# RWKV-7 recurrence and a mixture of 16 experts on one core: expert places of different widths, filled in order of the experts' counts

## The chip, the core and the metric

The kernel runs on one core of a Trainium2 chip. The core has a matrix engine (TensorE; PE in the profile, its weight loads PEld), three engines for element work (VectorE: DVE, ScalarE: ACT, GpSimd: POOL), a queue engine that starts loads and stores (SyncE: SP), and 16 DMA engines that move the data. Each engine works through its own list of instructions in order and waits on semaphores for the others. Matmuls read SBUF and write PSUM, 8 banks of 2 KB a partition. The metric is device time in microseconds, the median of several executions. All data are fp32; an fp32 matmul is recorded as two passes, each with its own weight load.

## The reference

First a recurrence over 768 steps for 4 x 8 heads of size 40, then a layer of 16 experts (4 groups of 4) over the 3072 tokens it gives. Each token goes to one expert, the best of its best group.

```python
for t in range(S):
    y[:, :, t] = np.einsum('bhd,bhde->bhe', rt, state)
    Sa = np.einsum('bhde,bhe->bhd', state, at)
    state_decay = state * wt[:, :, None, :] - np.einsum('bhd,bhe->bhde', Sa, bt)
    state = state_decay + np.einsum('bhd,bhe->bhde', vt, kt)
x = y.transpose(0, 2, 1, 3).reshape(B * S, H * D)        # 3072 x 320
g_idx = argmax(x @ w_group);  e_idx = argmax(xg @ w_expert[g])
h = np.maximum(xg[mask_e] @ w1[g, e], 0.0)               # 320 -> 1024
out[tok_idx] = (g_w * e_w)[:, None] * (h @ w2[g, e])     # 1024 -> 320
```

## The kernel before, in words

The first part (to about 420 us of the profile) computes the recurrence in chunks of 128 steps, 6 chunks, and writes x to memory (`x_nat`). While it runs, tokens are assigned: `choose` finds each token's expert (one-hot rows `oh`) and weight (`pay`), `rank_products` and `ranks` number the tokens within their expert, `table` and `table_products` turn this into a table `tab` that holds for each expert and each row the token's number and its weight, and `index` makes integers of it (`src_i` for gathering, `dst_i` for storing). `lift` sees to it that each expert has at least a first tile of 128 rows counted. The last of the six chunks is assigned in the tail.

In the second part, the tail, each of the 16 experts has a place of 240 rows: a first tile of 128 and a second of 112 (`CAP`, `TB2`, `WX`). Rows that no token fills are computed and not stored. Tokens beyond the 240th of an expert are marked in `ov`; if any is, or a guard of the recurrence trips, a slow path behind the tail (line 1154) runs, which is skipped in the profiled execution.

For expert e: `gather` (line 743, POOL) fetches the rows of x; `fill` (749, ACT) copies a remainder of 64 columns once more, so that it stands on both halves of the partitions; `turn_x_in` (755 to 758) transposes on PE and copies to `xTs`; `layer1` multiplies with w1: x has 320 = 128 + 128 + 64 columns, so line 772 does the two full parts for eight blocks of 128 hidden units, and line 780 the part of 64, two blocks at a time on the two row halves. The moving operand has the place's width, 240 columns, in a call. Half of the outputs get their relu on ACT (782), half on DVE (783). `layer2` then does for each of the two tiles eight matmuls of 320 columns (793), a scaling by the weight on DVE (799) and an indirect store (800, POOL).

The order on each engine is the order in which the program is written (lines 1061 to 1129). Experts 0 and 1 are interleaved with the assignment of the last chunk: `layer1(0, 0, P, "whole")` is the part of line 772 for expert 0's first tile, "rest" that of line 780. From expert 2 on a loop runs: gathers for e + 2, fills for e + 1, `layer1(e)`, transposes for e + 1, `layer2` for both tiles, weights for e + 3. Weights (2.62 MB an expert) are loaded by `load_weights` on SP into three buffers in turn; the loads wait until PE has read the buffer's last user. Experts come in the order 0 to 15.

PSUM banks are handed out in turn from two rings, "wide" (5 banks) and "thin" (3).

## Time and profile before

| | |
|---|---|
| median of 3 runs | 730.04 us (727.44 to 734.29) |
| profiled execution, device time | 731.19 us |
| its span, first to last instruction | 729.5 us |
| PE busy | 624.9 us (86% of the span) |
| PE weight loads busy | 533.2 us (73%) |
| DVE / ACT / POOL busy | 361.4 / 276.7 / 294.6 us |
| memory read and written | 74.41 and 9.50 MB |
| mean granted clock of PE | 0.941 of 2.4 GHz |

A row of the timeline is: start in us, duration in us, engine, line, operation, output <- inputs, shape, how many instructions were merged into the row, and in brackets the idle time before it and what ended it. A row of the windows view gives for each engine the busy time in a stretch and the number of instructions, then PE's granted clock as a share of 2.4 GHz, the share of time in which the DMA engines were busy, and the rate. The view of a line gives minimum, median and maximum duration in ns of all instructions of one program line. Matmuls overlap, so that the time of a pass is read from start to start and not from its own duration.

### The profile page before, as it was taken

The numbers are of one execution on the slowest core, as the hardware profiler recorded it, in microseconds if no ns is written. First come the engines' busy times: TensorE is split into PE (matmuls) and PEld (weight loads), VectorE is DVE, ScalarE is ACT, GpSimd is POOL, SyncE is SP. The second block draws the span as 40 slices with busy tenths as digits, with TensorE's granted clock in tenths as the row PEclk, the third lists the DMA queues.
The fourth block names the chain that finished last, engine by engine and source line by source line (L and its number), as shares of the span: only waits on it lengthen the run. The fifth ranks groups of instructions, "written<-read, shape, count | busy, mean of one in ns | idle before, by whom it ended". The sixth has DMA issues, their size and how long they took to land. (4 is left out here: it accounts for less than half of the span.)

```text
span 729.5 us, 26775 instructions
## 1 busy us (share of the span) xinstructions
PE 624.9 (86%) x11850; PEld 533.2 (73%) x11850; DVE 361.4 (50%) x631; ACT 276.7 (38%) x720; POOL 294.6 (40%) x415
## 2 busy tenths in 40 slices
PE   2642888888899889988879899999999999999993
PEld 2532777787788778877878786877777777777772
DVE  8799588778678778776714442111111111111110
ACT  6952966575685774762260310111111111111100
POOL 5110089779779879868200013222222222222111
PEclk9755689999999999999999999999999999999997
DMA  5540414245345344442253064755555555554000
GB/s 130 124 111 1 97 29 99 58 120 123 94 113 128 60 111 96 122 137 42 40 174 85 22 190 132 241 176 175 178 178 176 176 174 175 178 179 165 14 13 15
DMA packets 129103, 84.74 MB, mean 116 GB/s; under 512 B 77995, under 2 KB 121008, under 8 KB 128980
## 3 DMA queue, kind: packets, MB, share of 16 engines
q1 hardware_dynamic: 125908, 74.10, 36.9%
q0 software_dynamic: 3072, 8.85, 3.5%
q8 instruction: 95, 1.56, 0.9%
q14 instruction: 28, 0.23, 0.1%
HBM read 74.41 MB, written 9.50 MB: 115 GB/s over the span
## 5 line engine op out<-in xcount | busy, mean ns | idle before, releaser
L800 POOL DMA_INDIRECT out_dram<-homek,dst_i x32 | 31.8, 992 | 212.6 <-DVE homek L799 203.4
L481 POOL TENSOR_TENSOR home<-home,tmp 128x30 f32<-128x30 f32 (+9 forms) x150 | 110.3, 735 | 11.7
L479 POOL TENSOR_TENSOR tmp<-home,TT 128x30 f32<-128x30 f32 (+9 forms) x150 | 93.6, 624 | 11.4
L419 PE MATMUL nar<-home,home 64*128 64x128 f32 x768 | 69.0, 323 | 31.8 <-DVE home L387 15.0
L772 PE MATMUL nar<-homeg,home 128*128 128x240 f32 (+2 forms) x464 | 90.3, 347 | 0.0
L419 PEld LDWEIGHTS nar<-home,home 64*128 64x128 f32 x768 | 59.7, 224 | 37.4 <-issue 23.0
L772 PEld LDWEIGHTS nar<-homeg,home 128*128 128x128 f32 x464 | 79.0, 191 | 9.1 <-issue 3.3
L743 POOL DMA_INDIRECT homeq<-x_nat,src_i x32 | 31.2, 976 | 92.9 <-DVE pad L644 66.6
L543 PE MATMUL seq<-VN,homeg 64*64 64x40 f32 x768 | 50.8, 236 | 14.2 <-ACT RHS L547 9.4
L431 ACT COPY TT<-nar 32x256 f32<-32x256 f32 x96 | 34.7, 361 | 72.0 <-PE nar L419 37.7
L543 PEld LDWEIGHTS seq<-VN,homeg 64*64 64x64 f32 x768 | 44.4, 141 | 17.0 <-ACT RHS L547 10.7
L793 PE MATMUL one<-home,homeq 128*128 128x320 f32 (+1 forms) x192 | 53.4, 434 | 0.0
L799 DVE TENSOR_SCALAR homek<-one,tab 128x320 f32<-128x320 f32 (+1 forms) x22 | 12.1, 551 | 81.2 <-PE one L793 81.2
L545 PE MATMUL seq<-ST,home 64*64 64x40 f32 x768 | 50.2, 234 | 0.0
L592 DVE TENSOR_TENSOR MN<-nar,up 128x512 f32<-128x512 f32 x48 | 31.0, 687 | 36.6 <-PE nar L588 36.5
L793 PEld LDWEIGHTS one<-home,homeq 128*128 128x128 f32 (+1 forms) x192 | 34.8, 184 | 15.7 <-issue 0.3
L426 DVE TENSOR_TENSOR homeg<-nar,up 64x256 f32<-64x256 f32 x80 | 33.4, 418 | 24.5 <-ACT TT L432 14.5
L545 PEld LDWEIGHTS seq<-ST,home 64*64 64x64 f32 x768 | 44.6, 144 | 0.0
L793 PE MATMUL one<-home,DT 128*112 128x320 f32 (+1 forms) x160 | 44.5, 433 | 0.0
L782 ACT ACTIVATE DT<-nar 128x480 f32<-128x480 f32 (+1 forms) x13 | 7.5, 573 | 93.7 <-PE nar L780 62.5
L462 POOL TENSOR_SCALAR_AFFINE_SELECT TT<-TT 128x1024 f32<-128x1024 f32 x6 | 8.9, 1479 | 82.5 <-DVE TT L458 78.4
L782 ACT ACTIVATE homeq<-nar 128x480 f32<-128x480 f32 (+2 forms) x12 | 6.8, 570 | 91.0 <-PE nar L780 75.4
(209 smaller groups left out, 1291.2 us busy)
## 6 DMA issues: line engine op xcount, KB each, us to landing
home<-in_w_dram SPq DMA_DIRECT2D x16, 1280.0 KB
home<-in_w_dram SPq DMA_DIRECT2D x16, 1024.0 KB
home<-in_w_dram SPq DMA_DIRECT2D x32, 128.0 KB
home<-in_kT_dram SPq DMA_DIRECT2D x48, 80.0 KB
home<-in_bT_dram SPq DMA_DIRECT2D x48, 80.0 KB
home<-in_aT_dram SPq DMA_DIRECT2D x24, 160.0 KB
VN<-in_v_dram SPq DMA_DIRECT2D x48, 80.0 KB
home<-in_vT_dram SPq DMA_DIRECT2D x48, 80.0 KB
```

Of the source, the lines that this page charges most:

```text
L419: nc.tensor.matmul(ps[j][:, i, :], lhsT=KB[half(j), i0 + i, c2], rhs=At[half(j), 0:b + 1:b, :], start=True, stop=True)
L426: nc.vector.tensor_tensor(G[half(j), hs], ps[j][half(j), :, HW:], up2[half(j), None, :].broadcast_to([HW, NH, HW]), op=ALU.mult)
L431: nc.scalar.copy(out=TT[q:q + HB, ns], in_=ps[j][q:q + HB, :, HW:])
L479: eng.tensor_tensor(t3, W[:, r0:r2, s:s + 1].broadcast_to([P, m, n]), sub[:, s:s + 1, s + 1:].broadcast_to([P, m, n]), op=ALU.mult)
L481: eng.tensor_tensor(W[:, r0:r2, s + 1:], W[:, r0:r2, s + 1:], t3, op=ALU.subtract)
L543: nc.tensor.matmul(ps[half(1 - j), i, :], lhsT=self.G[half(j), i, :], rhs=self.VN[half(j), i, j, :], start=True, stop=False)
L545: nc.tensor.matmul(ps[half(1 - j), i, :], lhsT=self.At[half(j), 1 + 2 * i + self.c2, :], rhs=S0[half(j), i, :], start=False, stop=True)
L592: nc.vector.tensor_tensor(self.MN[:, j], ps[j], up2[:, None, :].broadcast_to([P, NI, HW]), op=ALU.mult)
L743: nc.gpsimd.indirect_dma_start(out=xt[:CAP[h], :DM], out_offset=None, in_=x_nat[:, :], in_offset=bass.IndirectOffsetOnAxis(ap=src_i[:CAP[h ...
L772: nc.tensor.matmul(ps[:, f, :], lhsT=w1s[:, ko, (g0 + f) * P:(g0 + f + 1) * P], rhs=xT[:, ko, :], start=(f == 0 and ko == 0), stop=False, ...
L793: nc.tensor.matmul(ps, lhsT=hts[e % 2][:, f, h * P:h * P + n], rhs=wbuf[e % 3][2][:, f, :], start=(k == 0), stop=(k == FQ - 1))
L800: nc.gpsimd.indirect_dma_start(out=out[:, :], out_offset=bass.IndirectOffsetOnAxis(ap=dst_i[:n, h, e:e + 1], axis=0), in_=yt[:n], in_offse ...
```

## The change

Places from the third on are no longer tied to an expert. Experts 0 and 1 keep the first two places; the other 14 are sorted by their number of tokens while the kernel runs, and fill places 2 to 15 in falling order. Each place has its own width, a constant of the program: 240 for places 0, 1 and 2, then 232, twice 224, twice 216, twice 208, and 192 for the last six. The second tile of a place has its width less 128 rows. In places of 192 it has 64, and there the eight matmuls of the second layer go alternately to output partitions 0 to 63 and 64 to 127 of one bank, two separate sums that ACT and DVE add afterwards.

What this needs is new code: `seen_by(NN)` counts all tokens, `order_experts` ranks the 14 experts by count (a matmul with ones, seven operations on DVE) and writes their numbers to `er_v`; `sort_tables` sorts the columns of `tab`; `overflow` computes `ov` from the widths; `load_expert` reads an expert's number from `er_v` into a register of SP, from which the loads' addresses are formed. The load for the third place, which stood at the head of the tail, stands behind `order_experts`. `ranks` has one operation less.

```diff
-    TB2 = 112
+    NF0 = 2
+    NV = NE - NF0
+    WIDTHS = [240] * (NF0 + 1) + [232] + [224] * 2 + [216] * 2 + [208] * 2
+    WIDTHS += [192] * (NE - len(WIDTHS))
...
-        for i, x in enumerate((0, P, P + TB2)):
-            nc.gpsimd.memset(thr[:, i:i + 1], float(x))
+        for i, x in enumerate(WIDTHS):
+            nc.gpsimd.memset(room_k[:, i:i + 1], float(x))
...
-            nc.vector.tensor_reduce(out=rank, in_=mine, axis=AX.X, op=ALU.add)
-            nc.vector.tensor_tensor(ge, rank[:, :, None].broadcast_to([P, n, 3]),
-                                    thr[:, None, :].broadcast_to([P, n, 3]), op=ALU.is_ge)
-            nc.vector.scalar_tensor_tensor(row[:, ms], ge[:, :, 1], -float(P), rank, op0=ALU.mult, op1=ALU.add)
-            nc.vector.tensor_tensor(hs, ge[:, :, :2], ge[:, :, 1:], op=ALU.subtract)
+            nc.vector.tensor_reduce(out=rank[:, ms], in_=mine, axis=AX.X, op=ALU.add)
+            nc.vector.tensor_single_scalar(hs[:, :, 1], rank[:, ms], float(P), op=ALU.is_ge)
+            nc.vector.scalar_tensor_tensor(row[:, ms], hs[:, :, 1], -float(P), rank[:, ms], op0=ALU.mult, op1=ALU.add)
+            nc.vector.tensor_scalar(hs[:, :, 0], hs[:, :, 1], -1.0, 1.0, op0=ALU.mult, op1=ALU.add)
...
-            nc.vector.tensor_copy(out=ov[:, ms], in_=ge[:, :, 2])
...
+        def order_experts():
+            pt = spot([P, NE])
+            nc.tensor.matmul(pt, lhsT=ones, rhs=seen, start=True, stop=True)
...
+            nc.vector.scalar_tensor_tensor(key, lane[:, NF0:NE], -1.0 / NE, pt[:, NF0:], op0=ALU.mult, op1=ALU.add)
+            nc.vector.tensor_tensor(more, key[:, None, :].broadcast_to(sq_v), key[:, :, None].broadcast_to(sq_v),
+                                    op=ALU.is_gt)
+            nc.vector.tensor_reduce(out=pos, in_=more, axis=AX.X, op=ALU.add)
+            nc.vector.tensor_tensor(sel, pos[:, None, :].broadcast_to(sq_v), lane[:, :NV, None].broadcast_to(sq_v),
+                                    op=ALU.is_equal)
+            nc.vector.tensor_tensor(more, sel, lane[:, None, NF0:NE].broadcast_to(sq_v), op=ALU.mult)
+            nc.vector.tensor_reduce(out=pos, in_=more, axis=AX.X, op=ALU.add)
+            nc.vector.tensor_copy(out=er_v, in_=pos)
+
+        def sort_tables():
...
+            nc.vector.tensor_tensor(big_t.rearrange("p (a k) e -> p a k e", a=4),
+                                    tab.rearrange("p a h e -> p (a h) e")[:, :, None, NF0:].broadcast_to(n4),
+                                    sel[:, None, :, :].broadcast_to(n4), op=ALU.mult)
+            nc.vector.tensor_reduce(out=srt.rearrange("p a h k -> p (a h k)"), in_=big_t, axis=AX.X, op=ALU.add)
+            nc.vector.tensor_scalar(src_v, srt[:, 0], float(NTOK - 1), None, op0=ALU.min)
+            nc.vector.tensor_copy(out=dst_v, in_=srt[:, 0])
+
+        def overflow():
...
+        def rows_of(e, h):
+            return WIDTHS[e] - P if h else P
...
+        def layer2(e, h):
+            n = rows_of(e, h)
+            ps = room([P, DM], "thin")
+            two = n <= HW
+            for k in range(FQ):
                 f = order[k]
-                nc.tensor.matmul(ps, lhsT=hts[e % 2][:, f, h * P:h * P + n], rhs=wbuf[e % 3][2][:, f, :],
-                                 start=(k == 0), stop=(k == FQ - 1))
+                nc.tensor.matmul(ps[half(k % 2, n)] if two else ps[:n], lhsT=hts[e % 2][:, f, h * P:h * P + n],
+                                 rhs=wbuf[e % 3][2][:, f, :], start=(k < 1 + two), stop=(k >= FQ - 1 - two),
+                                 skip_group_check=two)
...
+            if two:
+                nc.scalar.copy(out=yt[:n], in_=ps[half(1, n)])
+                nc.vector.tensor_tensor(yt[:n], ps[:n], yt[:n], op=ALU.add)
+                nc.vector.tensor_scalar(yt[:n], yt[:n], wt, None, op0=ALU.mult)
+            else:
+                nc.vector.tensor_scalar(yt[:n], ps[:n], wt, None, op0=ALU.mult)
...
+        def load_expert(e):
+            if e < NF0:
+                load_weights(e * DM, e * F, wbuf[e % 3])
+                return
+            er = nc.sync.value_load(er_v[0:1, e - NF0:e - NF0 + 1], min_val=NF0, max_val=NE - 1)
+            load_weights(nc.s_assert_within(er * DM, NF0 * DM, (NE - 1) * DM),
+                         nc.s_assert_within(er * F, NF0 * F, (NE - 1) * F), wbuf[e % 3])
...
         gate["tail"] = True
-        load_weights(2 * DM, 2 * F, wbuf[2])
...
         ranks(NF, B)
+        seen_by(NN)
         table(NF, B)
         layer1(0, 0, P, "rest")
+        order_experts()
+        load_expert(2)
         layer1(1, 0, P, "whole")
         table_products(NF)
         index(1)
         for e in range(2):
             gather(e, 1)
+        sort_tables()
         gather(2, 0)
         layer1(1, 0, P, "rest")
         layer2(0, 0)
+        overflow()
...
-            layer1(e, 0, WX)
+            layer1(e, 0, WIDTHS[e])
...
-                load_weights((e + 3) * DM, (e + 3) * F, wbuf[e % 3])
+                load_expert(e + 3)
```

Three places where the order of instructions moves, all in the tail between the first tiles of experts 0 and 1. On PE, before: the last two matmuls of "rest" of expert 0 (line 780), "whole" of expert 1 (772), then the table of the last chunk (704).

```order
L780 MATMUL nar_103<-homeg,home_110 128x128
L780 MATMUL nar_104<-homeg,home_110 128x128
L772 MATMUL nar_101<-homeg,home_111 128x128 [waits DVE_49]
L772 MATMUL nar_101<-homeg,home_111 128x128 x7
L772 MATMUL nar_102<-homeg,home_111 128x128 [waits Activation_49]
L772 MATMUL nar_102<-homeg,home_111 128x128 x7
L704 MATMUL nar_103<-Rr,first 128x32 [waits DVE_49,Activation_49]
L704 MATMUL nar_103<-Rr,first 128x32 x3
```

The same place on PE in the changed kernel, where line 829 is the old 780, 821 the old 772 and 708 the old 704.

```order
L829 MATMUL nar_107<-homeg,home_114 128x128
L829 MATMUL nar_108<-homeg,home_114 128x128
L729 MATMUL nar_105<-seen,ones 128x16 [waits DVE_49]
L821 MATMUL nar_106<-homeg,home_115 128x128 [waits Activation_49]
L821 MATMUL nar_106<-homeg,home_115 128x128 x7
L821 MATMUL nar_107<-homeg,home_115 128x128 [waits Activation_49]
L821 MATMUL nar_107<-homeg,home_115 128x128 x7
L708 MATMUL nar_108<-Rr,first 128x32 [waits DVE_49]
L708 MATMUL nar_108<-Rr,first 128x32 x3
```

One matmul that waits for `seen` on DVE (line 729) now stands ahead of expert 1, and each of the following outputs takes the next bank of the ring.

On DVE, before, from the end of the last chunk's ranks to its table's addition (711): the overflow copy (676), the two operations of `table`, and half of expert 0's relu (783).

```order
L676 COPY ov<-Rr 128x4
L691 TENSOR_TENSOR Rr<-hp,oh 128x128 [waits DVE_49]
L694 TENSOR_TENSOR first<-row,lane 128x512
L783 TENSOR_SCALAR DT_117<-nar_104 128x4x128 [waits PE_49]
L711 TENSOR_TENSOR tab<-tab,nar_103 128x2x16 [waits PE_49,Activation_49]
```

The same stretch of DVE in the changed kernel (644 is `seen_by`, 695 and 698 `table`, 832 the relu, 732 to 740 `order_experts`, 715 the old 711).

```order
L644 TENSOR_REDUCE seen<-oh 128x16
L695 TENSOR_TENSOR Rr<-hp,oh 128x128 [waits DVE_49]
L698 TENSOR_TENSOR first<-row,lane 128x512
L832 TENSOR_SCALAR DT_121<-nar_108 128x4x128 [waits PE_49]
L732 SCALAR_TENSOR_TENSOR small_7438<-lane,nar_105 128x14 [waits PE_49]
L733 TENSOR_TENSOR first<-small_7438 128x196 [waits DVE_49]
L735 TENSOR_REDUCE small_7439<-first 128x14 [waits DVE_49]
L736 TENSOR_TENSOR homek<-small_7439,lane 128x196 [waits DVE_49]
L738 TENSOR_TENSOR first<-homek,lane 128x196 [waits DVE_49]
L739 TENSOR_REDUCE small_7439<-first 128x14 [waits DVE_49]
L740 CAST er_v<-small_7439 128x14 [waits DVE_49]
L715 TENSOR_TENSOR tab<-tab,nar_108 128x2x16 [waits PE_49]
```

The count takes the place of the copy, and the seven operations of the ordering stand between the relu and the addition of the table.

On SP, before: the last store of x and the four loads for expert 2.

```order
L625 DMA x_nat<-xn 128x320 [waits DMAHW5_49,Activation_49]
L182 DMA home_112<-in_w_dram 128x2x1024 [waits DMAHW6_49,PE_49]
L184 DMA home_112<-in_w_dram 64x512 [waits DMAHW7_49,DVE_49,PE_49]
L184 DMA home_112<-in_w_dram 64x512 [waits DMAHW0_49]
L186 DMA home_112<-in_w_dram 128x8x320 [waits DMAHW1_49,DVE_49,PE_49]
```

On SP in the changed kernel, the same stretch (632 is the store, 189 to 193 the loads, ISA short register instructions).

```order
L632 DMA x_nat<-xn 128x320 [waits DMAHW5_49,Activation_49]
L862 TENSOR_LOAD er_v [waits DVE_49]
L862 ISA x2
L189 ISA
L189 DMA home_116<-in_w_dram 128x2x1024 [waits DMAHW6_49,PE_49]
L191 ISA
L191 DMA home_116<-in_w_dram 64x512 [waits DMAHW7_49,DVE_49,PE_49]
L191 ISA
L191 DMA home_116<-in_w_dram 64x512 [waits DMAHW0_49]
L193 ISA
L193 DMA home_116<-in_w_dram 128x8x320 [waits DMAHW1_49,DVE_49,PE_49]
```

Ahead of the loads SP reads the expert's number, which waits for DVE, and each load is preceded by a register instruction.

## Rows read from the trace of the kernel before

**Rows 1.** Windows: stretch, busy us (count) of each engine, clock, DMA, rate.

```profile
core 0: us, PE busy (x) PEld busy (x) DVE busy (x) ACT busy (x) POOL busy (x), PEclk, DMA share, GB/s
480.00:500.00 20.00, 20.00 (x95) 15.03 (x94) 3.14 (x7) 1.95 (x6) 4.96 (x5) 1.00 0.49 161
```

**Rows 2.** Timeline: PE in expert 2, to the first matmuls of expert 3.

```profile
465.55 3.40 PE L772 MATMUL nar<-homeg,home 128*128 128x240 f32 x16
...
468.89 1.08 PE L780 MATMUL nar<-homeg,home 64*128 64x240 f32 x8
...
469.90 1.89 PE L772 MATMUL nar<-homeg,home 128*128 128x240 f32 x8
...
475.02 4.48 PE L793 MATMUL one<-home,DT 128*128 128x320 f32 x16
...
483.65 3.40 PE L772 MATMUL nar<-homeg,home 128*128 128x240 f32 x16
```

**Rows 3.** Timeline: PE with tiles of 128 columns, experts 0 and 1.

```profile
428.26 1.16 PE L780 MATMUL nar<-homeg,home 64*128 64x128 f32 x16
...
429.35 3.84 PE L772 MATMUL nar<-homeg,home 128*128 128x128 f32 x32
...
433.02 0.98 PE L704 MATMUL nar<-Rr,first 128*128 128x32 f32 x8
```

**Rows 4.** Timeline: PE where outputs alternate between two column halves.

```profile
365.39 1.59 PE L614 MATMUL nar<-wsel,home 128*64 128x100 f32 x32
366.92 0.47 PE L507 MATMUL one<-X,TT 32*32 32x32 f32 x17
...
368.56 0.91 PE L614 MATMUL nar<-wsel,home 128*64 128x100 f32 x16
369.40 1.20 PE L521 MATMUL one<-DT,X 32*32 32x32 f32 x64
...
417.39 1.28 PE L605 MATMUL one<-MN,homek 128*40 128x64 f32 x31
418.46 0.25 PE L614 MATMUL nar<-wsel,home 128*64 128x100 f32 x1
```

**Rows 5.** Timeline: a small matmul with ones, and the end of the last ranks.

```profile
417.12 0.35 PE L643 MATMUL nar<-seen,ones 128*128 128x16 f32 x2
...
430.33 0.16 DVE L676 COPY ov<-Rr 128x4 f32<-128x4 f32 x1
```

**Rows 6.** One line's instructions: durations in ns (min/median/max), starts, shapes.

```profile
L637 DVE TENSOR_REDUCE seen<-oh x3: 474/584/693, 329.3 to 406.1; 128x16 f32<-128x192 f32 x1, 128x16 f32<-128x256 f32 x1, 128x16 f32<-128x320 f32 x1
...
L622 ACT COPY xn<-nar x24: 425/426/433, 151.3 to 421.4; 128x320 f32<-128x320 f32 x24
...
L582 DVE TENSOR_TENSOR ST<-ST,scale x10: 491/492/693, 129.0 to 354.2; 128x320 f32<-128x320 f32 x10
...
L1150 SPq TENSOR_LOAD <-loops x1: 735/735/735, 461.7 to 461.7; - x1
```

**Rows 7.** Timeline: expert 0's second tile, from fill to the first layer.

```profile
437.81 0.24 ACT L749 COPY homeq<-homeq 112x64 f32<-112x64 f32 x1 [2.09 <-DMA homeq<-x_nat,src_i]
...
443.74 0.45 PE L755 MATMUL nar<-ident,homeq 112*128 112x112 f32 x3
...
445.38 2.04 PE L772 MATMUL seq<-homeg,home 128*128 128x112 f32 x16 [1.19 <-DVE homeg L757]
```

**Rows 8.** Windows: PE's clock after an idle microsecond, and after rows 7.

```profile
391.00:392.00 1.00, 0.03 (x1) 0.00 (x0) 0.69 (x1) 0.00 (x0) 0.00 (x0) 1.00 0.05 11
...
394.00:395.00 1.00, 1.00 (x19) 0.96 (x20) 0.00 (x0) 0.21 (x1) 0.00 (x0) 0.51 0.00 0
...
397.00:398.00 1.00, 1.00 (x33) 1.00 (x31) 0.86 (x5) 0.00 (x0) 0.00 (x0) 0.78 0.00 0
...
445.00:450.00 5.00, 4.62 (x46) 4.51 (x48) 0.33 (x2) 0.25 (x1) 2.71 (x3) 1.00 0.31 96
```

**Rows 9.** Timeline: SP issues the first load for expert 2.

```profile
424.15 0.41 SPq L182 DMA_DIRECT2D home<-in_w_dram  x1
```

More of the change, by code (lines that the diff above doesn't have):

```diff
@@ L97 @@
     first_i = cpool.tile([P, G], F32, name="first_i")
-    thr = cpool.tile([P, 3], F32, name="thr")
+    room_k = cpool.tile([P, NE], F32, name="room_k")
+    rank = cpool.tile([P, NN], F32, name="rank")
+    src_v = cpool.tile([P, 2, NV], I32, name="src_v")
+    dst_v = cpool.tile([P, 2, NV], I32, name="dst_v")
+    er_v = cpool.tile([P, NV], I32, name="er_v")
     again = {B: cpool.tile([P, NE, B], F32, name="again")}
@@ L661, in ranks @@
                                for i, sh in enumerate(([P, NE, n], [P, NE, n], [P, n, NE])))
-            rank, ge, hs = (view(rl[:, i * NN:i * NN + w * n], sh)
-                            for i, w, sh in ((0, 1, [P, n]), (1, 3, [P, n, 3]), (4, 2, [P, n, 2])))
+            hs = view(rl[:, :2 * n], [P, n, 2])
             nc.vector.tensor_copy(out=slot, in_=ps[:, 1])
@@ new lines, in sort_tables @@
+        def sort_tables():
+            n4 = [P, 4, NV, NV]
+            big_t = view(first.rearrange(flat)[:, :4 * NV * NV], [P, 4 * NV, NV])
+            nc.vector.tensor_tensor(big_t.rearrange("p (a k) e -> p a k e", a=4),
[4 more added lines that the diff above has]
+            nc.vector.tensor_copy(out=dst_v, in_=srt[:, 0])
@@ new lines, in overflow @@
+        def overflow():
+            cap, mine = small_of([P, NE]), view(fl[:, :NN * NE], [P, NN, NE])
+            more = view(rl[:, :NV * NV], sq_v)
+            nc.vector.tensor_copy(out=cap[:, :NF0], in_=room_k[:, :NF0])
+            nc.vector.tensor_tensor(more, sel.rearrange("p k e -> p e k"), room_k[:, None, NF0:].broadcast_to(sq_v),
+                                    op=ALU.mult)
+            nc.vector.tensor_reduce(out=cap[:, NF0:], in_=more, axis=AX.X, op=ALU.add)
+            nc.vector.tensor_tensor(mine, oh, cap[:, None, :].broadcast_to([P, NN, NE]), op=ALU.mult)
+            nc.vector.tensor_reduce(out=ov, in_=mine, axis=AX.X, op=ALU.add)
+            nc.vector.tensor_tensor(ov, rank, ov, op=ALU.is_ge)
```

44 lines of the change are left out of this document (20 added, 24 removed).

## The prediction

> **What bounds the kernel now.** The windows view comes first: in it the reader compares PE's busy time with the length of the stretch and reads the granted clock. From 480 to 500 us PE is busy 20.00 of 20.00 us at a granted clock of 1.00 (2.4 GHz), while the transfers use 0.49 of the DMA engines [rows 1]. The chain of waits has only its last microsecond here, so I read the timeline of PE next, for the price of each part of one expert [rows 2]. Expert 2 takes 18.10 us from its first first-layer matmul (465.55) to expert 3's (483.65). The first 16 passes (an fp32 matmul is two passes of the array) of 240 columns take 468.89 - 465.55 = 3.34 us, 208.8 ns each; the eight passes of the 64-row remainder take 1.01 us; two such rounds make the first layer, about 8.8 us. The second layer, two tiles of 16 passes of 320 columns, takes 483.65 - 475.02 = 8.63 us, 4.31 a tile, the same for the tile of 128 rows and that of 112. So fourteen experts follow one another on a saturated PE, and what a place costs is the columns that PE streams there. A row that no token fills costs as much as a filled one.
>
> **Term 1, the first layer of narrower places.** Against 240, the places lose 8 columns (once), 16 (twice), 24 (twice), 32 (twice) and 48 (six times): 440 columns. Each column is streamed by 32 full passes of an expert and by the two rounds of remainder. No place has one of the new widths today, so I bound the price from both sides. At 128 columns 32 passes take 433.02 - 429.35 = 3.67 us, 114.7 ns each [rows 3]; between that and 208.8 ns at 240 lie 0.84 ns a column. Between 240 and the 269.7 ns at 320 [rows 2] lie 0.76. The remainder takes 1.01 us for 8 passes at 240 and 429.35 - 428.26 = 1.09 for 16 at 128, so 4.15 ns a column and round. Together 32 x 0.76 + 7.5 = 31.8 to 32 x 0.84 + 8.3 = 35.2 ns a column, 14.0 to 15.5 us for 440. I take 14.7: the new widths lie between the two pairs of points. Nothing hides PE's time here, and nothing that PE waits for is near (term 5), so this comes off the end in full.
>
> **Term 2, the second tile on two column halves.** In the last six experts the second tile has 64 rows, and its matmuls go alternately to output partitions 0 to 63 and 64 to 127. It is a gain only if two of them run at once. The kernel has this form already: line 614 multiplies 128 partitions into 64 output rows, alternating halves of one bank, 100 columns. Thirty-two passes take 366.92 - 365.39 = 1.53 us and sixteen 369.40 - 368.56 = 0.84 [rows 4]: 43.1 ns a further pass, and 0.15 us fixed for going into the form and out of it. One after the other, 100 columns at the slopes above would be about 80 ns, so they do run in pairs. For 320 columns that is 138 ns a pass in proportion, 16 x 0.138 + 0.15 = 2.36 us; taking half of 269.7 ns instead, 2.31. I take 2.33 against 4.31: 1.98 us saved, six times, 11.9. Line 605 is the less favourable row: 64 columns, two different right-hand sides, 31 passes in 418.46 - 417.39 = 1.07 us, 34.5 ns each [rows 4], 0.54 ns a column against 0.43. At that price a tile takes 2.91, and six save 8.4. I lean to line 614, whose 64 rows and 100 columns are nearer. A lower bound of nothing saved would need line 614's pairs to be absent.
>
> The Trainium skill, "TensorE: Matmul & The Clock Gate", section "Measured speedup vs the span model", gives three column tiles a speedup of 2.38 and not 3. By that proportion two halves are worth 1.59 (an estimate from that page): 4.31 becomes 2.71, six tiles save 9.6, and the sum ends 2.3 us later. It would be right if that shortfall goes with each pair; line 614 shows none.
>
> **Term 3, a new wait at the head of the tail.** The count of all tokens (`seen_by(NN)`) now stands on VectorE behind the ranks of the last chunk, and a matmul with it stands on PE between "rest" of expert 0 and "whole" of expert 1. Today PE begins the latter at 429.35 [rows 3], and VectorE has the ranks done only with the copy at 430.33 [rows 5]. `ranks` has one operation less, so the reduction starts where that copy stands. Its price: line 637 takes 474, 584 and 693 ns for 192, 256 and 320 elements a partition [rows 6], so 0.80 us for 384, ending at 431.13. Then come 0.1 us of handing over and the two passes of the small matmul, 0.27 us (417.12 to 417.39, [rows 4, 5]). PE goes on at 431.5 and not 429.35: **+2.1 us**, and all behind it on PE moves by that. PE has no slack later to take it up: its next gap, 1.19 us before 445.38 [rows 7], is a round trip over VectorE that moves along. Lower bound 1.8, should the small operations run closer. Upper bound: PE's clock. At 391 us PE was idle nearly a whole microsecond, and from 394 to about 397.5 the granted clock was half (1.2 GHz) [rows 8]: 3.5 us at half speed lose 1.75 of work. Yet the gap of 1.19 us left the clock at 1.00 [rows 7, 8]. I leave it out of the sum and keep 3.9 as the upper end.
>
> **Term 4, the end.** The last tile's output now needs an ACT copy of one half (320 columns out of PSUM, 0.43 us by line 622), a VectorE addition in place of the scaling, and the scaling after it (0.49 us by line 582, 128 partitions; here 64) [rows 6]. With two hand-overs **+1.0 us**, bounds 0.7 and 1.3. The five tiles before it have the next expert's 7 us of PE work over them.
>
> **Term 5, what I put at nothing, and its cover.**
> VectorE in the tail: ordering the experts is seven small operations, five of 196 elements; by line 637's 1.71 ns an element about 0.34 each plus gaps, some 2.4 us after PE's small matmul, done at 434. They stand before the addition of the table, which waits for PE until about 436 anyway. `sort_tables`, two operations of 784 elements (at most 1.34 each) and two tiny ones, ends near 440 and has queued behind it the second half of expert 1's relu. That half is first used by the third matmul of expert 1's second layer, which starts near 441.5 (443.74 less the 4.31 of a tile, [rows 7], plus 2.1). The cover is about a microsecond; beyond it PE waits.
> Gathers: expert 0's second tile is gathered about 2 us later; today its fill runs at 437.81 and PE uses it at 443.74 [rows 7], which also moves by 2. Cover 5.9 us.
> The load of expert 2 was issued at 424.15 [rows 9]; now SP reads a register first (735 ns and two short steps, as at line 1150, [rows 6]) and that waits for the order: about 435. Nothing but loads is queued behind it on SP. The weights (2.62 MB) are needed at 467.6, 32 us later; at the 161 GB/s that half-busy DMA engines move in [rows 1] they take 16. Each later load starts about 1 us later on SP, and is issued more than two experts ahead of its use.
> Bandwidth: the narrow experts take about 18.1 - 1.6 - 2.0 = 14.5 us, so the same bytes raise the share from 0.49 to about 0.61.
> The constants add thirteen one-column memsets on POOL early in the recurrence; `overflow`, six operations (two of 384 elements) in place of a copy, follows expert 0's first output on VectorE, about 442 to 444.7; expert 1's first output, which queues behind it, comes at 445.8 (today 443.7, [rows 7]).
>
> **Sum.** -14.7 - 11.9 + 2.1 + 1.0 = -23.5 us. The profiled execution took 731.19 us (span 729.5), so 707.7; it stood 1.15 us over the median of the three runs (730.04), on which the sum gives 706.5. I predict **707 us**.
>
> **The rivals.**
> (a) The halves overlap only in part, at line 605's price: six tiles save 8.4 and not 11.9, +3.5, **711 us**. For it: different right-hand sides stream at once, as here. Against it: its rows are only 40 wide and its passes so short that a fixed cost a pass would give the same number. The figure of the Trainium skill named under term 2 would give a time between, 709. Chance 0.17.
> (b) The head costs more: the new wait lowers PE's clock (+1.75), or the relu behind `sort_tables` comes late by a microsecond: **709 to 710 us**. For it: [rows 8]; against it: the gap of 1.19 us, which changed nothing. Chance 0.20.
> (c) Slower than before: the loads, whose addresses now come from a register, become the bound. No load in this trace does that. It decides from the point where one expert's 2.62 MB and its 0.5 MB of gathered and stored rows take more than the mean place, 18.1 - 26.6/14 = 16.2 us, that is below 193 GB/s; slower than before from below about 172 GB/s (18.1 us). At 100 GB/s thirteen experts of 31 us would add some 170 us, about **900**. Against it: the rate is that of the DMA engines, which the address does not change, and [rows 1] has them half idle. Chance 0.02.
> (d) The change doesn't do what it says: an expert overflows its place, and the slow path behind the loop runs, at tens of microseconds. The reference's inputs give counts of 204 and 162 for the first two, and sorted 229, 213, 213, 211, 203, 202, 198, 197, 189, 180, 178, 174, 167, 152 for the rest; each fits, the tightest 189 in 192. Chance 0.01.
>
> **How the numbers follow.** My forecast has 0.60, (a) 0.17, (b) 0.20, (c) and (d) 0.03. Best terms together (15.5, 12.1, 1.8, 0.7) give 706.1 on the profiled time, 704.9 on the median; the three runs of before spread by 3.5 us to either side of their middle, so the low end is 702. The high end takes (a) and (b) singly, 711, with 2 us for the same spread: 713. A difference of 1% (7.3 us) is about what a measurement of this kernel can tell from none; only (c), (d) or a total failure of terms 1 and 2 come to within it or above: faster 0.94, same 0.03, slower 0.03.
>
> **What would show it.** Per place, first-layer passes of 192 columns near 167 ns and an expert at 192 near 14.5 us. Sixteen passes of the 64-row tile in 2.3 us: 4.3 says no overlap, 2.9 rival (a). One PE gap of about 1.9 us before "whole" of expert 1, with the granted clock at 1.00 after it or at half. SP's four loads of expert 2 near 435, and PE never waiting for one. After the last matmul about 1 us more to the last store. The prediction fails if PE has waits between experts that are not there today, or if a 64-row tile costs what a 112-row tile does.

## The result, and the profile after

The changed kernel takes 708.43 us (median of 4 runs, 706.45 to 710.17) against 731.37 us for the kernel before on the same chip (4 runs, 727.44 to 734.29): a ratio of 0.969, 95% interval 0.963 to 0.975. The forecast was 707 us with a range of 702 to 713. The time fell inside, but part of that agreement is luck, as the traces show: the errors of the sum, 3.4 us on balance, are half hidden by 1.8 us in a part of the program for which nothing was forecast.

The span of the profiled execution fell from 729.5 to 707.6 us. It is best cut at one group of instructions that both programs have: the 16 passes of 64 rows of expert 0 (line 829, 780 before). Ahead of them lies the recurrence, in which the change only makes `ranks` shorter by an operation and adds some memsets; behind them lies nearly all that it touches. In the kernel before they start at 428.26 [rows 3], so 301.2 us lie behind them. After, the timeline of PE at that place (start, us, engine, line, operation, tile, shape, count, and in brackets the idle time ahead of it) reads:

```profile
426.46 1.16 PE L829 MATMUL nar<-homeg,home 64*128 64x128 f32 x16
429.37 0.40 PE L729 MATMUL nar<-seen,ones 128*128 128x16 f32 x2 [1.75 <-DVE seen L644]
429.62 5.45 PE L821 MATMUL nar<-homeg,home 128*128 128x128 f32 x32
434.90 0.98 PE L708 MATMUL nar<-Rr,first 128*128 128x32 f32 x8
...
441.31 4.47 PE L842 MATMUL one<-home,homeq 128*128 128x320 f32 x16
```

From 426.46 to the end, at 707.6, are 281.1 us: **the tail is 20.1 us shorter**, not 23.5. The other 1.8 us lie ahead, in the recurrence (428.26 to 426.46), and were in no term of the sum (see the section on the head below).

The new wait stands where it was expected: L829 to L821 takes 3.16 us and not 1.09 [rows 3], +2.07. What was not in the sum is the line behind it. The 32 passes of 128 columns take 434.90 - 429.62 = 5.28 us, where they took 3.67 [rows 3]: +1.61. The windows view (the clock is the number before the last two) shows why:

```profile
428.00:429.00 1.00, 0.00 (x0) 0.00 (x0) 0.93 (x5) 0.25 (x1) 0.00 (x0) 1.00 0.00 0
429.00:430.00 1.00, 0.63 (x5) 0.63 (x6) 1.00 (x3) 0.00 (x0) 0.00 (x0) 0.95 0.00 0
430.00:431.00 1.00, 1.00 (x6) 1.00 (x6) 0.96 (x4) 0.00 (x0) 0.00 (x0) 0.50 0.00 0
...
433.00:434.00 1.00, 1.00 (x9) 1.00 (x9) 0.00 (x0) 0.00 (x0) 0.00 (x0) 0.84 0.00 0
```

PE was idle for 1.75 us. In the microsecond in which its work comes back the granted clock is still 0.95; then it is 0.50 (1.2 GHz) until some way into 433 to 434, about 3.4 us.

Narrow places of 192 columns, on the timeline of PE, with one row of its weight loads (PEld); the first of them starts at 607.09:

```profile
607.09 2.76 PE L821 MATMUL nar<-homeg,home 128*128 128x192 f32 x16
609.78 0.92 PE L829 MATMUL nar<-homeg,home 64*128 64x192 f32 x8
610.63 2.87 PE L821 MATMUL nar<-homeg,home 128*128 128x192 f32 x16
613.43 0.92 PE L829 MATMUL nar<-homeg,home 64*128 64x192 f32 x8
614.28 0.55 PE L804 MATMUL seq<-ident,homeq 128*128 128x128 f32 x3
...
619.59 1.81 PEld L842 LDWEIGHTS one<-home,DT 128*64 128x64 f32 x16 [0.44 <-issue]
619.59 2.37 PE L842 MATMUL one<-home,DT 128*64 128x320 f32 x16
621.90 2.87 PE L821 MATMUL nar<-homeg,home 128*128 128x192 f32 x16
624.69 0.92 PE L829 MATMUL nar<-homeg,home 64*128 64x192 f32 x8
...
629.19 0.87 PE L804 MATMUL nar<-ident,homeq 128*128 128x128 f32 x6
630.00 4.57 PE L842 MATMUL one<-home,homeq 128*128 128x320 f32 x16
634.50 2.37 PE L842 MATMUL seq<-home,homeq 128*64 128x320 f32 x16
636.81 2.87 PE L821 MATMUL nar<-homeg,home 128*128 128x192 f32 x16
```

The place that starts at 621.90 takes 636.81 - 621.90 = 14.91 us against 18.10 [rows 2]. Its first layer takes 629.19 - 621.90 = 7.29 (that of the first narrow place 614.28 - 607.09 = 7.19), and the 64-row tile in this stretch 636.81 - 634.50 = 2.31. But the six transposes take 630.00 - 629.19 = 0.81, and the tile of 128 rows, which the diff does not touch, takes 4.50 where it took 4.31 [rows 2]. PE does not wait anywhere in this stretch, and the transfers use 0.61 of the DMA engines there (0.49 in [rows 1]):

```profile
616.00:640.00 24.00, 24.00 (x136) 17.30 (x136) 4.51 (x10) 2.87 (x10) 5.85 (x6) 1.00 0.61 195
```

At the end, the last tile's halves are added and stored (timeline, all engines but the weight loads):

```profile
688.83 6.88 PE L842 MATMUL one<-home,homeq 128*128 128x320 f32 x32
695.76 0.42 ACT L849 COPY homek<-one 64x320 f32<-64x320 f32 x1 [6.27 <-PE one L842]
696.21 0.48 DVE L850 TENSOR_TENSOR homek<-one,homek 64x320 f32<-64x320 f32 x1 [2.22 <-ACT homek L849]
...
697.54 0.91 POOL L854 DMA_INDIRECT out_dram<-homek,dst_v  x1 [2.29 <-DVE homek L851]
```

From PE's end (688.83 + 6.88 = 695.71) to the store are 1.83 us. In the kernel before, the same way runs through one scaling:

```profile
709.59 8.88 PE L793 MATMUL one<-home,homeq 128*128 128x320 f32 x32
...
718.51 0.55 DVE L799 TENSOR_SCALAR homek<-one,tab 112x320 f32<-112x320 f32 x1 [3.76 <-PE one L793]
719.33 0.95 POOL L800 DMA_INDIRECT out_dram<-homek,dst_i  x1 [3.31 <-DVE homek L799]
```

That is 719.33 - 718.47 = 0.86; the end costs +0.97.

### The profile page after: what moved, and what is told of

It reads as the page before. It is cut to its first block, busy times and chain, and to the rows that moved or that the text cites. A ratio compares the mean times of both kernels' runs of the same rounds, so it can differ in the third digit from the quotient of the medians.

```text
span 707.6 us, 26969 instructions
## 1 busy us (share of the span) xinstructions
PE 601.4 (85%) x11852; PEld 513.3 (73%) x11852; DVE 367.5 (52%) x651; ACT 277.2 (39%) x726; POOL 295.3 (42%) x428
## 5 line engine op out<-in xcount | busy, mean ns | idle before, releaser
L486 POOL TENSOR_TENSOR tmp<-home,TT 128x30 f32<-128x30 f32 (+9 forms) x150 | 103.5, 690 | 11.4
L488 POOL TENSOR_TENSOR home<-home,tmp 128x30 f32<-128x30 f32 (+9 forms) x150 | 100.9, 672 | 11.8
L854 POOL DMA_INDIRECT out_dram<-homek,dst_v x28 | 27.7, 990 | 170.7 <-DVE homek L853 156.6
L821 PE MATMUL nar<-homeg,home 128*128 128x192 f32 (+7 forms) x472 | 84.5, 333 | 1.2 <-DVE homeg L806 1.2
L821 PEld LDWEIGHTS nar<-homeg,home 128*128 128x128 f32 x472 | 76.9, 195 | 7.8 <-issue 4.7
L842 PE MATMUL one<-home,homeq 128*128 128x320 f32 (+5 forms) x192 | 49.5, 436 | 0.0
L433 DVE TENSOR_TENSOR homeg<-nar,up 64x256 f32<-64x256 f32 x80 | 33.4, 418 | 23.9 <-ACT TT L439 16.0
L842 PEld LDWEIGHTS one<-home,homeq 128*128 128x128 f32 (+5 forms) x192 | 30.3, 172 | 16.1 <-issue 1.1
L842 PE MATMUL one<-home,DT 128*128 128x320 f32 (+4 forms) x160 | 40.6, 435 | 0.0
L792 POOL DMA_INDIRECT homeq<-x_nat,src_i x4 | 4.6, 1151 | 82.2 <-DVE pad L651 63.8
L853 DVE TENSOR_SCALAR homek<-one,homek 128x320 f32<-128x320 f32 (+4 forms) x15 | 8.2, 550 | 57.9 <-PE one L842 57.9
L595 PE MATMUL nar<-home 64*64 64x64 f32 x1536 | 31.7, 221 | 5.9 <-issue 5.7
```

Of the source, the lines that this page charges most:

```text
L433: nc.vector.tensor_tensor(G[half(j), hs], ps[j][half(j), :, HW:], up2[half(j), None, :].broadcast_to([HW, NH, HW]), op=ALU.mult)
L486: eng.tensor_tensor(t3, W[:, r0:r2, s:s + 1].broadcast_to([P, m, n]), sub[:, s:s + 1, s + 1:].broadcast_to([P, m, n]), op=ALU.mult)
L488: eng.tensor_tensor(W[:, r0:r2, s + 1:], W[:, r0:r2, s + 1:], t3, op=ALU.subtract)
L595: nc.tensor.matmul(ps[j][half(h), i, :], lhsT=self.VT[half(j), i, h, :], rhs=self.R[half(j), i, self.ts], start=True, stop=True)
L821: nc.tensor.matmul(ps[:, f, :], lhsT=w1s[:, ko, (g0 + f) * P:(g0 + f + 1) * P], rhs=xT[:, ko, :], start=(f == 0 and ko == 0), stop=False, ...
L842: nc.tensor.matmul(ps[half(k % 2, n)] if two else ps[:n], lhsT=hts[e % 2][:, f, h * P:h * P + n], rhs=wbuf[e % 3][2][:, f, :], start=(k < ...
```

## The experiments

All of them start from the changed kernel. Behind each label stands the tail of its profiled execution, from the start of L829's 16 passes (a line number moves by one or three where lines were added or taken out) to the end of the span. It is steadier than the whole time: two executions of the changed kernel have tails of 281.1 and 281.2 us, while the part ahead took 426.46 us in one and 422.98 in the other.

### Without the halves: e1_no_halves

```diff
-            two = n <= HW
+            two = False
```

> The changed kernel with the two column halves undone: the 64-row tiles of the last six places run all 16 passes into partitions 0 to 63, one after the other; widths and order stay. Theory (two halves run in pairs, and the gain is the pairing): the 64-row tile takes 4.3 to 4.5 us instead of 2.31, the end loses its addition (-1.0), so 708.4 + 12.3 - 1.0 = about 720 us, ratio to before about 0.984. Rival (a tile of 64 rows is cheaper by itself, pairing adds little): its 16 passes take well under 4 us and the time stays under 714. A second question: the first tile of 128 rows takes 4.50 us in these places and 4.31 elsewhere; if that is a change of the array's form ahead of 64-row outputs, it stays 4.50 here.

718.5 us, ratio 0.987 (0.981 to 0.993); tail 293.0 us, **+11.9** on the changed kernel. The pairing is the gain, and it is nearly complete:

```profile
630.57 0.87 PE L804 MATMUL nar<-ident,homeq 128*128 128x128 f32 x6
631.38 4.57 PE L842 MATMUL one<-home,homeq 128*128 128x320 f32 x16
635.88 4.52 PE L842 MATMUL seq<-home,homeq 128*64 128x320 f32 x16
640.33 2.87 PE L821 MATMUL nar<-homeg,home 128*128 128x192 f32 x16
```

The same 64-row tile takes 640.33 - 635.88 = 4.45 us one after the other, 2.31 in pairs: a factor of 1.93. The reader should also see that the transposes (0.81) and the 128-row tile (4.50) are as slow here as with halves. So the halves do not slow their neighbours; something that both kernels share does.

### All places 240 wide: e2_all_240

```diff
-    WIDTHS = [240] * (NF0 + 1) + [232] + [224] * 2 + [216] * 2 + [208] * 2
-    WIDTHS += [192] * (NE - len(WIDTHS))
+    WIDTHS = [240] * NE
```

> The changed kernel with every place at 240: counting, sorting, register-addressed loads and the new wait stay, narrower places and halves are gone. Theory: what is left is the cost alone, 2.1 us for PE's wait for the count and 1.6 for the half clock after it, so before + 3.7 = about 735 us, ratio 1.005, and each expert from the third on takes 18.1 us as before. Rival (sorting and register loads cost more, spread over the experts): experts longer than 18.1 us or waits of PE between them, 740 us or more. Second rival (the wait is covered): 731 us.

730.0 us, ratio 1.003 (0.999 to 1.006). With all widths as before, and so no tile of 64 rows, what is left is the counting, the order, the sorted tables and the loads by register. PE's wait for the count (1.76 us) and the slow passes behind it (5.45) stand in its trace as in that of the changed kernel. The tail has 304.8 us, **+3.6** on the kernel before. The wait and the clock make 2.07 + 1.61 = 3.68, so nothing else in this part of the change costs anything in the tail. By the tail alone the whole time would be 0.5% longer; the measured 0.3% has that in its interval, as it has the 0% of the second rival. The trace tells the two apart.

### The order worked out later: e3_order_later, e3_again

```diff
         layer1(0, 0, P, "rest")
-        order_experts()
-        load_expert(2)
         layer1(1, 0, P, "whole")
...
             gather(e, 1)
+        order_experts()
+        load_expert(2)
         sort_tables()
```

> The changed kernel with the matmul and the seven operations of the ordering, and the load for the third place, moved behind the table of the last chunk and the two gathers that follow it; nothing else. Theory: PE no longer waits for the count, the clock stays at 1.00, expert 1's 32 passes take 3.67 us again and not 5.28: 3.7 us less than the changed kernel, about 704.7 us (ratio to before 0.964). The gather of expert 0's second tile, which landed 8.2 us after its issue while the third place's weights were loading, lands in about 3 us. Rival (the wait only moves): VectorE's sorting now stands ahead of expert 1's relu with nothing in between, PE waits for that relu in expert 1's second layer, and the time stays at 707 or above.

> e3_order_later once more. From the same 16 passes to the end 277.8 us, 3.3 us less than the changed kernel. If the part ahead varies from execution to execution only, the median comes out about 3.3 us under that of after_again (ratio 0.0045 lower); if working out the order later makes the part ahead longer (it took 428.9 us in the one trace), the two medians are equal.

703.1 us, ratio 0.966 (0.961 to 0.970), and 705.0 us, 0.967 (0.964 to 0.970), in a second set of runs, beside which the changed kernel itself stood at 706.6 us, 0.969 (0.966 to 0.973). The tail is 277.8 us in both traces, **-3.4**. Wait and clock are both gone:

```profile
428.90 1.16 PE L829 MATMUL nar<-homeg,home 64*128 64x128 f32 x16
429.99 3.84 PE L821 MATMUL nar<-homeg,home 128*128 128x128 f32 x32
433.67 0.98 PE L708 MATMUL nar<-Rr,first 128*128 128x32 f32 x8
434.48 0.38 PE L729 MATMUL nar<-seen,ones 128*128 128x16 f32 x2
```

L829 to L821 is 1.09 us again and the 32 passes take 3.68. The small matmul costs its 0.30 us and no wait, since the reduction has ended long before. The load of the third place starts at 438.81 instead of 434.11, and nothing waits for it. In the whole time less of the gain shows than in the tail: the second median lies 0.0023 of the ratio under the changed kernel's, half-way between the two values that were set against each other (see the section on the head).

### Work in the gap: e7_fill_gap

```diff
+            bk = spot([P, 2 * P])
+            for _ in range(8):
+                nc.tensor.matmul(bk[:, P:], lhsT=ones, rhs=ones, start=True, stop=True)
+            pt = bk[:, :NE]
             nc.tensor.matmul(pt, lhsT=ones, rhs=seen, start=True, stop=True)
```

> The changed kernel with eight matmuls of ones by ones, 128 columns (their sums are read by nobody), ahead of the matmul that waits for the count, 1.8 us of PE work for a wait of 1.75. Theory (PE's idleness drops the clock): the granted clock stays 1.00, expert 1's 32 passes take 3.67 us and not 5.28, the small matmul starts no later: 1.6 us less, about 706.8 us. Rival (the clock falls for another reason, or the 5.28 us come from something else): the passes still take about 5.3 us and the time is unchanged, 708.4.

705.6 us, ratio 0.972 (0.966 to 0.978); tail 280.1 us, **-1.1**.

```profile
424.33 2.05 PE L730 MATMUL nar<-ones 128*128 128x128 f32 x16
...
426.42 3.82 PE L824 MATMUL nar<-homeg,home 128*128 128x128 f32 x32
430.07 0.98 PE L708 MATMUL nar<-Rr,first 128*128 128x32 f32 x8
```

Eight multiplications whose sums nobody reads fill the gap. The path is no shorter (from the 16 passes at 423.24 to L824 at 426.42 is 3.18 us, as before the edit), but the clock stays at 1.00 and the 32 passes behind it take 3.65 us instead of 5.28. So at this place the idle PE is what lowered the clock, and the lower clock cost the 1.6 us. Half a microsecond of it is lost again some 20 us later: the transposes of expert 1's second tile wait 0.91 us for ACT's copy of their rows, 0.41 in the changed kernel. That copy queues behind a relu, which starts 0.6 us after the last of its matmuls and not 0.1 (447.85 after 447.26, against 452.19 after 452.09); why it does was not followed further.

### Loads that need no register: e4_static_loads

```diff
-            if e < NF0:
-                load_weights(e * DM, e * F, wbuf[e % 3])
-                return
-            er = nc.sync.value_load(er_v[0:1, e - NF0:e - NF0 + 1], min_val=NF0, max_val=NE - 1)
-            load_weights(nc.s_assert_within(er * DM, NF0 * DM, (NE - 1) * DM),
-                         nc.s_assert_within(er * F, NF0 * F, (NE - 1) * F), wbuf[e % 3])
+            load_weights(e * DM, e * F, wbuf[e % 3])
```

> Each place from the third on loads the weights of the expert of its own number, at addresses fixed when the program is built; the tokens stay in sorted places, so this kernel leaves out reading the order back into a register, and its outputs belong to other weights. The load of the third place no longer waits for the order and starts about 10 us earlier (near 424 to 426 instead of 434.1). Theory (loads addressed by a register are hidden): no difference to the changed kernel beyond 1 us, ratio 0.965 to 0.971, because no instruction of TensorE in the changed kernel's trace waits for weights; the gather that now lands 8.2 us after its issue should land after about 3 us again, which moves nothing, since its fill was not waited for. Rival (the register loads cost something per place): faster than the changed kernel by 3 us or more, ratio under 0.963.

707.9 us, ratio 0.972 (0.967 to 0.977, its middle a thousandth above what was expected); tail 281.2 us, +0.1. The register-addressed loads cost nothing that shows in the tail, and rival (c) falls. What did change is the gather of expert 0's second tile. In the changed kernel it is issued at 436.79 and the copy that fills the tile comes at 445.01, 0.6 us ahead of its use on PE (0.24 us in after_again: 441.90 and 442.14). Here (POOL's and ACT's timeline) the issue and the fill are 3.4 us apart:

```profile
434.02 1.50 POOL L792 DMA_INDIRECT homeq<-x_nat,src_i  x1 [17.70 <-DVE src_i L720]
437.43 0.24 ACT L798 COPY homeq<-homeq 112x64 f32<-112x64 f32 x1 [2.60 <-DMA homeq<-x_nat,src_i]
```

and in the changed kernel 8.2 us:

```profile
436.79 1.51 POOL L792 DMA_INDIRECT homeq<-x_nat,src_i  x1 [17.69 <-DVE src_i L720]
445.01 0.24 ACT L798 COPY homeq<-homeq 112x64 f32<-112x64 f32 x1 [7.42 <-DMA homeq<-x_nat,src_i]
```

In the seven traces in which the load of the third place is issued beside this gather it takes 6.0 to 8.6 us. Where that load is out of the way, earlier as here or later as in e3_order_later (435.63 to 438.62), it takes 3.0 to 3.4. So it was the load beside it that held it up.

### Second tiles of 72 rows: e5_last_200

```diff
-    WIDTHS += [192] * (NE - len(WIDTHS))
+    WIDTHS += [200] * (NE - len(WIDTHS))
```

> The last six places are 200 columns wide instead of 192, so their second tiles have 72 rows and go without the two column halves. Against the changed kernel: +1.6 us for 48 more columns (8 x 6 x 33.4 ns), +11.0 us for the halves lost (five x 2.0 and 1.0 in the last place, whose end gets shorter by 0.96). Theory (a 64-row second tile itself slows its neighbours: 128-row tile 4.50 us instead of 4.32, 64-row tile 4.45 instead of 4.31, six transposes 0.81 instead of 0.65): with 72 rows these come back to 4.32, 4.31 and 0.66 to 0.70, about -0.33 us a place against the changed kernel, so 718 to 720 us, ratio about 0.984. Rival (narrow places make their neighbours slow, whatever the rows): 128-row tile stays at 4.50 us, 721 us, ratio about 0.987. The trace tells the two apart by the duration of the 128-row tile.

716.8 us, ratio 0.981 (0.976 to 0.987); tail 291.2 us, **+10.1** (expected +10.6).

```profile
630.03 0.74 PE L804 MATMUL nar<-ident,homeq 128*128 128x128 f32 x6
630.60 4.52 PE L842 MATMUL one<-home,homeq 128*128 128x320 f32 x16
634.69 2.30 PEld L842 LDWEIGHTS seq<-home,homeq 128*72 128x72 f32 x9
634.96 2.32 PE L842 MATMUL seq<-home,homeq 128*72 128x320 f32 x8
```

The transposes fall to 0.57 us and the 128-row tile to 4.36 (4.32 was expected), in a place only 8 columns wider. It is not the narrow place that slows them but the number 64. The weight loads show it: here the first load of the 72-row tile starts at 634.69, 0.27 us ahead of its pass at 634.96, beside the last passes of the tile before. In the changed kernel the first load of the 64-row tile and its first pass both start at 619.59, after 0.44 us without a load.

### Transposes over 72 rows: e6_turn_72

```diff
-            pt = room([P, NK, n], "wide")
+            m = max(n, HW + 8)
+            pt = room([P, NK, m], "wide")
...
-                nc.tensor.transpose(pt[:, ko, :], xt[:n, ko * P:(ko + 1) * P], ident[:n, :n])
+                nc.tensor.transpose(pt[:, ko, :], xt[:m, ko * P:(ko + 1) * P], ident[:m, :m])
...
```

> Only the transposes of 64-row tiles are changed: they run over 72 rows (8 rows of rests that nobody reads), the halves stay. Theory (each form with 64 rows or 64 columns pays for its own change of form): the six transposes of a place fall from 0.81 to about 0.67 us, the 128-row tile stays at 4.50 us, -0.8 us in all, ratio about 0.968 if the changed kernel stands at 0.969. Rival (the 64-row transposes are what slows the 128-row tile behind them): that tile falls to 4.32 us too, -1.9 us in all, ratio about 0.966.

705.5 us, ratio 0.967 (0.962 to 0.972); tail 279.5 us, **-1.6**.

```profile
628.57 0.74 PE L805 MATMUL nar<-ident,homeq 128*128 128x128 f32 x6
629.14 4.52 PE L843 MATMUL one<-home,homeq 128*128 128x320 f32 x16
633.59 2.37 PE L843 MATMUL seq<-home,homeq 128*64 128x320 f32 x16
635.90 2.87 PE L822 MATMUL nar<-homeg,home 128*128 128x192 f32 x16
```

Neither expectation is right in its parts. The transposes fall from 0.81 to 0.57 us, nearly twice what was expected of them, and the 128-row tile from 4.50 only to 4.45. So of the 0.19 us that this tile lost, 0.05 came from the 64-row transposes ahead of it. Of the other 0.14, 0.09 go with the 64-row tile behind it, since e5_last_200, which has neither, stands at 4.36; the last 0.05 are in e5_last_200 too, and what they come from is not shown. More rows, which nobody reads, are cheaper here than fewer.

### Both together: e8_later_72, e8_again

The edits of e3_order_later and e6_turn_72.

> The order of the experts is worked out after the tail's gathers (as in e3_order_later) and the transposes of 64-row tiles run over 72 rows (as in e6_turn_72). Theory: the gains add, -3.4 us for the wait and the clock that e3_order_later took away and -0.8 us for the transposes: ratio 0.963 to 0.965, 702 to 704 us. Rival (the later load of the third place costs what the wait gave): ratio of the changed kernel, 0.968 to 0.969.

> e8_later_72 once more. From the same 16 passes to the end 276.3 us, 4.9 us less than the changed kernel: ratio 0.0065 under that of after_again if the part ahead varies from execution to execution only; equal to after_again if the later order makes the part ahead longer (428.2 us in the one trace).

705.5 us, ratio 0.969 (0.965 to 0.973), and 703.3 us, 0.962 (0.958 to 0.965), in the second set of runs, beside the changed kernel at 0.969 (0.966 to 0.973). The tails are 276.3 and 276.0 us, **-5.0**: there the gains add, and it is the shortest tail found. The whole times do not agree with each other: the first ratio is the rival's value and no better than that of e6_turn_72 beside it (0.967), the second is what the theory had. How much of the 5 us is left in the whole time is therefore open (see the next section).

### The head, and what the times can tell: after_again

> The changed kernel once more, beside the two kernels below on the same chip. From the start of the 16 passes of L829 ahead of the wait to the end of the span it took 281.1 us; the same 281 us is expected here, whatever the part ahead of it takes, which in ten executions so far took 423.2 to 428.9 us with the same instructions. Ratio 0.969 to 0.973.

706.6 us, ratio 0.969; tail 281.2 us, and 422.98 us ahead of it. The program ahead of L829 is the same in the changed kernel and in e3_order_later, yet thirteen traces of before, after and the experiments have it start between 422.98 and 429.34 us. PE's granted clock in the recurrence differs between them too, but it does not put them in order: from 120 to 180 us it is 1.00 in the kernel before (428.26 us ahead of the tail), 0.97 in the changed kernel (426.46), and 0.86 both in e3_order_later (428.90) and in e1_no_halves (425.69).

If each run's tail is taken as long as its kernel's traces have it, the part ahead of it can be estimated for every run. Over the three chips on which the experiments ran its mean is 425.5 us in 38 runs of the kernel before, 423.8 in 36 runs of the changed kernel and of the experiments that leave the ordering in its place, and 425.7 in 25 runs with the later order. Single runs scatter by about 2.4 us. The first two means differ by 1.7 us (0.6 to 2.7), the last two by 1.9 (0.5 to 3.2), and both differences have the same sign on each of the three chips. So the part ahead seems to be shorter in the changed kernel, which the prediction put at nothing, and the later order seems to give back a part of what its tail gains, although it moves only instructions behind L829. What does either is not shown, and nothing that sets the length or the clock of the recurrence was tried. A difference of 2 us in the whole time is hard to see in a few runs, and plain in the tail of a single trace; but the tail leaves out what happens ahead of it.

## Why the prediction was nearly right

**The total.** -23.5 us was forecast for the part that the change touches, -20.1 came. Another 1.8 us between the two traces lay ahead of that part, where no term stood; that the whole came to within 2 us of the forecast is in part their doing. The sum as it should have been:

| term | forecast, us | measured, us | from |
|---|---|---|---|
| narrower places | -14.7 | -11.8 | tails of e1_no_halves and e2_all_240 |
| halves, net of the end | -10.9 | -11.9 | tails of after and e1_no_halves |
| wait at the head of the tail | +2.1 | +2.07 | L829 to L821 |
| clock behind the wait | 0 | +1.61 | the 32 passes of L821 |
| sum | -23.5 | -20.0 | tail, before to after: -20.1 |

**Term 1 had the columns right and left out what a 64-row tile costs its neighbours.** The first layer takes 7.19 us in the first place of 192, behind a tile of 80 rows, and 8.79 in a place of 240 (464.44 to 473.23 in e2_all_240): 1.60 us for 48 columns, 33.3 ns a column where 33.4 was taken, or 14.7 us for the 440. Its first 16 passes take 609.78 - 607.09 = 2.69 us, 168 ns each (167 was forecast). The step that failed is the premise that a narrower place changes nothing but its columns. A 64-row tile lengthens what stands around it: the six transposes by 0.13 us (0.68 in e2_all_240), the 128-row tile by 0.19, itself, unpaired, by 0.14 (4.45 and 4.31), and the first 16 passes behind it by 0.10 (624.69 - 621.90 = 2.79). In the six places these make some 3.3 us; the transposes of the seven places before them, which are a little shorter than at 240, give 0.4 back, and what is left is the distance from 14.7 to 11.8. In e5_last_200, with 72 rows in that tile, the first layer takes 7.46 us in all six places, 33.3 ns a column again. Term 2 had a fixed 0.15 us for going into the form and out of it, and put all of that into the tile itself; the transposes, which go through a form of their own, were not in the sum at all. A sign of it stood in the kernel before: its first layer takes 8.79 us and not twice 3.34 + 1.01, because the second 16 passes, behind a remainder of 64 rows, take 3.44 (578.47 to 581.91 in a later expert; in a narrow place 613.43 - 610.63 = 2.80).

The Trainium skill has a rule that bears on it: "TensorEngine Tiling (Array Packing)", section "Key Properties", states that changing the tiling mode, and not just the tile, drains TensorE. The weight loads agree (a load 0.27 us ahead of its pass at 72 rows, none ahead at 64). The same page of the Trainium skill, section "When to Use Tiling", gives column tiling for up to 64 columns of the stationary operand; e5_last_200 and e6_turn_72 agree: 64 columns cost the change and 72 do not. The price, 0.09 to 0.14 us for a tile of 320 columns ahead of the change, 0.10 for 16 passes of 192 behind it and 0.24 for six transposes, stands only in the traces.

**Term 2 was right.** 2.33 us was forecast for a tile, 2.31 measured. That the halves gained 11.9 us net and not 10.9 is because the same tile, one pass after the other, takes 4.45 us and not 4.31; the difference stands against them in term 1. (Its 80 ns for 100 columns one after the other is 91 by the straight line through the points at 128 and 240; the 43.1 ns read from line 614 is about half of either.) Line 614 was the row to lean on, and rival (a), at line 605's price of 2.91, falls. So does the proportion of the three column tiles in the Trainium skill ("TensorE: Matmul & The Clock Gate", section "Measured speedup vs the span model"), by which 2.71 was estimated: two halves of 320 fp32 columns run 1.93 times as fast as one after the other.

**Term 3 was right in its size and wrong in its choice.** 0.80 us was forecast for the reduction and 0.78 came; +2.1 for the path, +2.07 came. But the clock was left out because a gap of 1.19 us had done nothing [rows 7, 8], although the nearest row the other way, an almost idle microsecond with a fall to half speed behind it [rows 8], stood beside it with its price. The length of a gap could not have settled it: in the same trace a gap of 1.87 us in the recurrence, ahead of 125.13, leaves the clock at 1.00 (the lines stand at the end of this text). Rival (b), with a chance of 0.20, was the case that came true in its first half: 1.75 us was its price, 1.61 the measured one. The other half of rival (b), a late relu, did not happen: it runs at 438.73, and the tile that needs it starts at 441.31 without a wait.

**Term 4 was right**: +1.0 forecast, +0.97 measured.

**Term 5 held, once only just.** The loads start at 434.11 to 436.70 (about 435 was forecast; the register read takes 0.27 to 0.48 us there and not 0.74) and PE waits for none; the DMA share in the narrow places is 0.61, as forecast. But the cover of the gather was taken to stay 5.9 us. The step that failed is that the load of the third place, moved from 424 to 434, now runs beside it; 0.6 us of cover were left (0.24 in after_again). It cost nothing, by that much.

## What to carry to other kernels

Price a new tile shape with its neighbours: the instruction before and the one after a change of the array's form pay too, and a few unused rows that keep the form can be cheaper than the exact size. A wait on a saturated PE costs its length and can cost a stretch at half clock behind it (here 2.07 and 1.61 us), and the length of the gap alone does not tell whether it will; move the small operation that waits to a place where its input is long ready, or put work into the gap. Where a part of the program varies from run to run, cut the traces at an instruction that both kernels have and compare the parts behind it, and check over many runs that the part ahead is the same.

## What the hardware showed beyond expectation

In the tail, a gap of 1.75 us on PE was followed by about 3.4 us at a granted clock of 0.50 in all seven traces that have the wait unfilled (after, after_again, e1_no_halves, e2_all_240, e4_static_loads, e5_last_200 and e6_turn_72: the row of the 32 passes shows the same 5.45 us in each), and the later gap of 1.19 us by none. That is no rule of length. In the recurrence of the kernel before a gap of 1.87 us leaves the clock at 1.00 (1.84 in the changed kernel does, too), and a gap of 1.87 us at the same place in e4_static_loads is followed by 0.50. Why is not shown. Timeline and windows, first before, then e4_static_loads:

```profile
125.13 1.08 PE L598 MATMUL one<-home,Sn 64*64 64x64 f32 x29 [1.87 <-ACT home L570]
125.00:130.00 5.00, 4.87 (x198) 4.63 (x200) 3.65 (x6) 3.69 (x9) 4.53 (x7) 1.00 0.10 18
...
123.18 1.08 PE L605 MATMUL one<-home,Sn 64*64 64x64 f32 x29 [1.87 <-ACT home L577]
125.00:126.00 1.00, 1.00 (x37) 0.88 (x34) 0.12 (x1) 0.99 (x3) 0.84 (x3) 0.50 0.06 16
```

A gather issued while a load of 2.62 MB started beside it took 6.0 to 8.6 us from issue to fill (8.2 in the changed kernel) instead of 2.8 to 3.4. And 64 rows cost more than 72: six transposes take 0.81 us against 0.57.
